# Sliding-window attention and a gated conv FFN on one core: q and k turned on VectorE, scores on 32-row tiles, two blocks per ScalarE and VectorE operation, the conv shared out among four engines, every queue's order from a table

## The chip, the cores and the metric

The kernel runs on one core of one Trainium2 chip. Five engines work side by side, each with an instruction queue of its own: TensorE (PE, matmuls into PSUM, which has eight banks of 128 x 512 f32 here), VectorE (DVE), ScalarE (ACT), GpSimd (POOL) and SyncE (SP), whose queue here issues the DMAs. The metric is the device time of one execution in microseconds; lower is better.

## What is computed

Eight batches of eight heads attend within a window of 32 positions to either side; the result goes through a feed-forward block whose gate is a three-tap convolution along the sequence.

```python
# q, k, v: 8 x 8 x 576 x 64 f32
scores = q @ k.T / sqrt(64)
mask = abs(pos[:, None] - pos[None, :]) <= 32
attn = softmax(where(mask, scores, -1e9))
x = (attn @ v).transpose(0, 2, 1, 3).reshape(8, 576, 512)
# w_in: 512 x 1024, conv_w: 3 x 1024, w_out: 1024 x 512
h = maximum(x @ w_in, 0)
conv = conv_w[0]*h[s-1] + conv_w[1]*h[s] + conv_w[2]*h[s+1]    # zero at the ends
out = (h * sigmoid(conv)) @ w_out                              # 8 x 576 x 512 f32
```

Both kernels take the sigmoid as (1 + tanh(conv/2)) / 2: the relu gives h/2, so the conv of it is conv/2, and the gate is one operation, (tanh + 1) * h/2.

## The kernel before

**Attention.** Batch by batch, two heads (a pair, `g`, 32 in all) at a time. `load_qk` (L99 to L106) brings four heads of q or k as f32 into 128 partitions, 18 rows of one head in each; `cast` (L109) turns them to bf16 on GpSimd. `job_tr` (L210) turns them: nine matmuls against the identity (L229) put 64 columns of two heads into three PSUM banks (`slot_a`, of which there is one), and one ScalarE and one VectorE copy (L236) bring the two pairs' halves out as `qT` and `kT`, with the head's 64 columns on 64 partitions. `job_sc` (L252) multiplies: nine query tiles of 64 rows against 128 keys each, for both heads of the pair, 18 matmuls on 64-row tiles (L257), again into `slot_a` (the last tile into a bank of its own). ScalarE takes the exponential of 1088 columns (L266) and of 64 (L267), VectorE multiplies with a 0/1 mask (L268). `job_av` (L270) multiplies with V, which has a column of ones for the softmax sum. V is kept twice, `ve` and, moved by 64 rows, `vo`; for batch 0 the move is VectorE's, for the others `shift_v` makes it with two DMAs (L136). A reciprocal (L292) and a multiplication (L301) on VectorE divide by the sum into `xn`. `job_xt` (L306) turns `xn` into `xT`: on TensorE for batches 0 and 1, with DMA transposes (L312) after that.

**Feed-forward.** The 4608 rows are 12 chunks of 384; three chunks lie on two batches. Per chunk and per block `m` of 128 of the 1024 hidden columns: `job_ph` (L339) runs four matmuls with `w_in` (L349) and ScalarE's relu (L360, L364, L369); `job_pc` (L371) runs the conv as three matmuls with diagonal matrices `diag_w` (L387), ScalarE's tanh from PSUM to an f32 tile in SBUF (L391), and VectorE's gate `(tn + 1) * hT` into `gT` (L392). `job_py` (L401) multiplies with `w_out`, eight matmuls for 128 rows (L405), ScalarE copies the result out (L410) and a DMA stores it (L412). Chunk 1 is done in two halves.

**Order.** Each job has a due time, written out by hand for the first batches and in a steady rhythm after that, and the jobs that must come ahead of it. `give_out` (L428) issues jobs by due time as soon as those ahead are issued. Up to a due time of 37 the instructions are held in that order on their engines (`InOrder`; these have line L87 in the profile); the DMAs and GpSimd's casts always; after that a scheduler of the framework may move instructions. Five PSUM banks (`slot_f`) rotate among the other jobs.

Of the kernel before, what the change touches and what calls it, by code (L numbers as in the profile page):

```python
# [10 lines left out]
BF16 = mybir.dt.bfloat16  # L12
AF = mybir.ActivationFunctionType
ALU = mybir.AluOpType


@with_exitstack
def kernel(
# [19 lines left out]
    NP = H // 2  # L38
# [4 lines left out]
    RP = S // 64  # L43

    consts = ctx.enter_context(tc.tile_pool(name="consts", bufs=1))
    pp = ctx.enter_context(tc.tile_pool(name="pp", bufs=1))
    apool = ctx.enter_context(tc.tile_pool(name="apool", bufs=3))
    fpool = ctx.enter_context(tc.tile_pool(name="fpool", bufs=2))
    spool = ctx.enter_context(tc.tile_pool(name="spool", bufs=3))
    psum_a = ctx.enter_context(tc.tile_pool(name="psum_a", bufs=1, space=bass.MemoryType.PSUM))  # L50
    psum_f = ctx.enter_context(tc.tile_pool(name="psum_f", bufs=5, space=bass.MemoryType.PSUM))

    NLD = 2
    NPH = NP // 2
    qkst = [[pp.tile([128, 2, RP, 64], FP32, name=f"{n}st{i}") for i in range(NPH)] for n in "qk"]
    vst = pp.tile([128, NBLK, H, 64], FP32, name="vst")
    qkb_pp = [
        [[pp.tile([128, RP, 2, 64], BF16, name=f"{n}b{i}{j}") for j in range(NPH)] for n in "qk"]
        for i in range(NLD)
    ]  # L60
    ve_pp = [pp.tile([128, NBLK, H, 65], BF16, name=f"ve{i}") for i in range(NLD)]
    vo_pp = [pp.tile([128, NBLK - 1, H, 65], BF16, name=f"vo{i}") for i in range(NLD)]
    NKT = 4
    kT_pp = [pp.tile([128, S + 2 * PAD], BF16, name=f"kT{i}") for i in range(NKT)]
    hT_pp = [pp.tile([128, MB, CH + (4 if i == 1 else 2)], BF16, name=f"hT{i}") for i in range(3)]

    w_in_sb = consts.tile([128, KC, d_ff], BF16, name="w_in_sb")
    w_out_sb = consts.tile([128, MB, d_model], BF16, name="w_out_sb")
    conv_w_sb = consts.tile([128, 3, MB], FP32, name="conv_w_sb")
    diag_w = consts.tile([128, 3, MB, 128], BF16, name="diag_w")  # L70
    ident = consts.tile([128, 128], BF16, name="ident")
    mask = consts.tile([128, 2 * S], BF16, name="mask")
    mask1 = consts.tile([128, NT, 64], BF16, name="mask1")

    fixed = tc.keep_in_program_order

    class InOrder:


        on = False  # L80

        def __init__(self, engine):
            self.engine = engine

        def __getattr__(self, name):
            do = getattr(self.engine, name)
            return (lambda *args, **kwargs: fixed(do(*args, **kwargs))) if InOrder.on else do  # L87

    vector, scalar, tensor = InOrder(nc.vector), InOrder(nc.scalar), InOrder(nc.tensor)

    def load_v(b, c):

        lo = 128 * c - PAD
        s0, s1 = max(0, lo), min(S, lo + 128)
        fixed(nc.sync.dma_start(  # L95
            vst[s0 - lo:s1 - lo, c, :, :], v[b, :, s0:s1, :].rearrange("h p d -> p h d")
        ))

    def load_qk(b, y, i):  # L99


        src = (q, k)[y][b, 4 * i:4 * i + 4, :, :]
        fixed(nc.sync.dma_start(
            qkst[y][i].rearrange("p e j d -> p e (j d)"),
            bass.AP(src.tensor, src.offset, [[RP * D, 128], [2 * S * D, 2], [1, RP * D]]),
        ))  # L106

    def cast(out_, in_):
        fixed(nc.gpsimd.tensor_scalar(  # L109
            out=out_, in0=in_, scalar1=1.0, scalar2=0.0, op0=ALU.mult, op1=ALU.add  # L110
        ))

    def load_stream(b):

        i = b % NLD
        ve, vo = ve_pp[i], vo_pp[i]

        def cast_v(c):
            cast(ve[:, c, :, 0:64], vst[:, c, :, :])
            if b == 0 and c > 0:  # L120
                vector.tensor_copy(vo[0:64, c - 1, :, :], ve[64:128, c - 1, :, :])
                vector.tensor_copy(vo[64:128, c - 1, :, :], ve[0:64, c, :, :])

        of_qk = [
            (lambda y=y, j=j: load_qk(b, y, j),
             lambda y=y, j=j: cast(qkb_pp[i][y][j].rearrange("p j e d -> p e j d"), qkst[y][j]))
            for j in range(NPH) for y in range(2)
        ]
        of_v = [(lambda c=c: load_v(b, c), lambda c=c: cast_v(c)) for c in range(NBLK)]
        return of_qk + of_v  # L130

    def shift_v(b):

        ve, vo = ve_pp[b % NLD], vo_pp[b % NLD]
        for p0, src in ((0, ve[64:128, 0:NBLK - 1]), (64, ve[0:64, 1:NBLK])):
            fixed(nc.sync.dma_start(vo[p0:p0 + 64], src))  # L136


    nc.vector.memset(vst[0:PAD, 0, :, :], 0.0)
    nc.vector.memset(vst[128 - PAD:128, NBLK - 1, :, :], 0.0)  # L140
    loads0 = list(load_stream(0))
    for ld, _ in loads0:
        ld()
    conv_w24 = consts.tile([3 * MB, 128], FP32, name="conv_w24")
    nc.scalar.dma_start(conv_w24, moe_conv_w.rearrange("k (m p) -> (k m) p", p=128))
    make_identity(nc, ident)
    ident24 = consts.tile([3 * MB, 3 * MB], FP32, name="ident24")
    nc.vector.tensor_copy(out=ident24, in_=ident[0:3 * MB, 0:3 * MB])
    nc.vector.memset(mask1, 1.0)
    nc.gpsimd.affine_select(  # L150
        out=mask1, in_=mask1, compare_op=ALU.is_ge, fill=0.0, base=0,
        pattern=[[0, NT], [-1, 64]], channel_multiplier=1,
    )
    nc.gpsimd.affine_select(
        out=mask1, in_=mask1, compare_op=ALU.is_ge, fill=0.0, base=64,
        pattern=[[0, NT], [1, 64]], channel_multiplier=-1,
    )
    nc.vector.memset(mask1[0:PAD, 0, :], 0.0)
    nc.vector.memset(mask1[128 - PAD:128, NT - 1, :], 0.0)
    for e in range(2):  # L160
        nc.vector.tensor_copy(
            out=mask[:, 512 * e:512 * e + 512], in_=mask1[:, 0:8, :].rearrange("p t x -> p (t x)")
        )
        nc.vector.tensor_copy(out=mask[:, 1024 + 64 * e:1088 + 64 * e], in_=mask1[:, 8, :])
    for t_ in ve_pp + vo_pp[0:1]:
        nc.vector.memset(t_[:, :, :, 64], 1.0)
    for t_ in kT_pp:
        nc.vector.memset(t_[:, 0:PAD], 0.0)
        nc.vector.memset(t_[:, PAD + S:], 0.0)
    nc.vector.memset(hT_pp[0][:, :, 0], 0.0)  # L170
    nc.vector.memset(hT_pp[1][:, :, HW + 1:HW + 3], 0.0)
    nc.vector.memset(hT_pp[2][:, :, CH + 1], 0.0)
    def make_diag(m):
        for kk in range(3):
            vector.tensor_scalar(
                out=diag_w[:, kk, m, :], in0=ident,
                scalar1=conv_w_sb[:, kk, m:m + 1], scalar2=None, op0=ALU.mult,
            )

    def load_weight(src, dst, rows, cast_):  # L180

        n = src.shape[1] // 2
        for x in (0, n):
            st = {}

            def load(x=x, st=st):
                t_ = fpool.tile([128, rows * n], FP32, name="wst", tag="wst")
                st[0] = t_.rearrange("p (c f) -> p c f", c=rows)
                fixed(nc.sync.dma_start(
                    st[0], src.rearrange("(c p) f -> p c f", p=128)[:, :, x:x + n]  # L190
                ))

            def casts(x=x, st=st):
                step = 512 // n
                for c in range(0, rows, step):
                    cast_(dst[:, c:c + step, x:x + n], st[0][:, c:c + step])

            yield load, casts


    def slot_a():
        return psum_a.tile([128, 1536], FP32, name="pa", tag="pa")

    def slot_f():
        return psum_f.tile([128, 512], FP32, name="pf", tag="pf")

    xT, xn = {}, {}
    state = {}

    def job_tr(g2, y):  # L210

        b, i = g2 // NPH, g2 % NPH
        nat = qkb_pp[b % NLD][y][i]
        to = []
        for g in (2 * g2, 2 * g2 + 1):
            if y == 0:
                t_ = apool.tile([128, S], BF16, name="qT", tag="qT", bufs=4)
                to.append(t_)
            else:
                t_ = kT_pp[g % NKT]  # L220
                to.append(t_[:, PAD:PAD + S])
            state["qk"[y], g] = t_

        small = b == 0
        for js in ((range(0, 4), range(4, 8), range(8, RP)) if small else (range(RP),)):
            j0, n = js[0], len(js)
            ps = slot_f() if small else slot_a()
            for j in js:
                tensor.matmul(  # L229
# [353 lines left out]
```

## Time and profile before

| | |
|---|---|
| median of 3 runs | 274.07 us (273.72 to 276.27) |
| span of the profiled execution | 271.7 us |
| PE busy | 236.4 us, 87% |
| ACT busy | 175.3 us, 65% |
| DVE busy | 160.5 us, 59% |
| POOL busy | 81.0 us, 30% |
| read from HBM, written | 32.52 MB, 9.44 MB |

The profile is of one execution. PE is the engine's matmuls, PEld its weight loads, which overlap them; a matmul's record holds its way through the array, so records in a row overlap, and the time of a job is read from starts. A group of the profile is named by line, engine, operation and tiles (`out<-in`), with the count, the busy time and the mean of one. In a timeline a line has the start, the duration and in brackets the idle time ahead of it with what ended it.

### The profile page before, as it was taken

The numbers are of one execution on the slowest core, as the hardware profiler recorded it, in microseconds if no ns is written. First come the engines' busy times: TensorE is split into PE (matmuls) and PEld (weight loads), VectorE is DVE, ScalarE is ACT, GpSimd is POOL, SyncE is SP. The second block draws the span as 40 slices with busy tenths as digits, with TensorE's granted clock in tenths as the row PEclk, the third lists the DMA queues.
The fourth block names the chain that finished last, engine by engine and source line by source line (L and its number), as shares of the span: only waits on it lengthen the run. The fifth ranks groups of instructions, "written<-read, shape, count | busy, mean of one in ns | idle before, by whom it ended". The sixth has DMA issues, their size and how long they took to land.

```text
span 271.7 us, 6447 instructions
## 1 busy us (share of the span) xinstructions
PE 236.4 (87%) x2535; PEld 143.5 (53%) x2562; DVE 160.5 (59%) x362; ACT 175.3 (65%) x370; POOL 81.0 (30%) x96
## 2 busy tenths in 40 slices
PE   1736974786999978998999999999999999999994
PEld 1625543574665544554555556565656455555551
DVE  5797385895466673765766656676666562323230
ACT  2755572585577663876777777777778567657552
POOL 5758656873026201233323432322300000000000
PEclk9999998998999997999999999999999999999998
DMA  7999999997377986399959988967546114312123
GB/s 258 256 344 358 198 296 321 224 309 164 100 183 253 222 151 165 110 287 242 208 146 319 159 196 257 294 112 177 152 121 89 40 41 109 98 39 77 41 77 116
DMA packets 70498, 49.64 MB, mean 183 GB/s; under 512 B 53676, under 2 KB 55748, under 8 KB 70468
## 3 DMA queue, kind: packets, MB, share of 16 engines
q1 hardware_dynamic: 70432, 49.22, 70.6%
q8 instruction: 20, 0.33, 0.6%
q14 instruction: 10, 0.08, 0.1%
q10 hardware_dynamic: 36, 0.01, 0.0%
HBM read 32.52 MB, written 9.44 MB: 154 GB/s over the span
## 4 chain that ended last, share of the span: by engine, by line
PE 68%; DMA 15%; DVE 5%; SPq 4%; ACT 3%; issue 2%; POOL 0%
PE pf L405 22%; PE pf L349 20%; PE pf L387 14%; DMA kst<-in_k_dram 5%; PE pa L229 4%; DMA vst<-in_v_dram 4%; PE pf L282 4%; DMA vo<-ve 3%; PE pa L257 3%; DMA xT<-xn 3%; SPq L95 2%; DVE attn L268 1%; SPq L312 1%; DVE gT L392 1%; DVE diag_w L87 1%
## 5 line engine op out<-in xcount | busy, mean ns | idle before, releaser
L392 DVE SCALAR_TENSOR_TENSOR gT<-tn,hT 128x384 bf16<-128x384 f32 (+1 forms) x96 | 55.7, 585 | 55.7 <-ACT tn L391 55.6
L349 PE MATMUL pf<-xT,w_in_sb 128*128 128x385 bf16 (+2 forms) x380 | 73.6, 317 | 4.9 <-DMA xT<-xn 3.7
L405 PE MATMUL pf<-w_out_sb,gT 128*128 128x512 bf16 x261 | 66.5, 385 | 1.7 <-issue 0.4
L387 PE MATMUL pf<-hT,diag_w 128*128 128x384 bf16 (+1 forms) x288 | 59.0, 314 | 0.7 <-ACT hT L360 0.6
L349 PEld LDWEIGHTS <-w_in_sb 128*128 128x128 bf16 x380 | 34.4, 98 | 25.9 <-issue 3.3
L410 ACT COPY y_sb<-pf 128x512 f32<-128x512 f32 x36 | 21.1, 586 | 40.8 <-PE pf L405 40.8
L391 ACT ACTIVATE tn<-pf 128x384 f32<-128x384 f32 (+1 forms) x96 | 44.9, 469 | 2.3 <-PE pf L387 1.9
L109 POOL TENSOR_SCALAR ve<-vst 128x512 bf16<-128x512 f32 x40 | 28.9, 724 | 55.2 <-DMA vst<-in_v_dram 42.9
L405 PEld LDWEIGHTS <-gT 128*128 128x128 bf16 x288 | 28.0, 99 | 30.4 <-issue 1.6
L387 PEld LDWEIGHTS <-diag_w 128*128 128x128 bf16 x288 | 26.1, 98 | 17.1 <-issue 1.2
L369 ACT ACTIVATE hT<-pf 128x385 bf16<-128x385 f32 x56 | 27.7, 496 | 10.8 <-PE pf L349 10.1
L266 ACT ACTIVATE attn<-pa 128x1088 bf16<-128x1088 f32 x26 | 27.9, 1074 | 4.7 <-PE pf L257 3.9
L109 POOL TENSOR_SCALAR qb<-qst 128x1152 bf16<-128x1152 f32 x16 | 19.9, 1242 | 26.8 <-DMA qst<-in_q_dram 26.8
L268 DVE TENSOR_TENSOR attn<-attn,mask 128x1152 bf16<-128x1152 bf16 x26 | 20.9, 804 | 10.4 <-ACT attn L267 9.6
L109 POOL TENSOR_SCALAR kb<-kst 128x1152 bf16<-128x1152 f32 x16 | 18.9, 1182 | 21.9 <-DMA kst<-in_k_dram 21.1
L301 DVE TENSOR_TENSOR xn<-pf,rec 128x320 bf16<-128x320 f32 x52 | 24.3, 486 | 0.8
L364 ACT ACTIVATE hT<-pf 128x386 bf16<-128x386 f32 x24 | 11.9, 494 | 4.4 <-PE pf L349 4.0
L282 PEld LDWEIGHTS <-attn 128*64 128x64 bf16 x520 | 10.7, 112 | 7.3 <-issue 5.6
L282 PE MATMUL pf<-ve,attn 128*64 128x65 bf16 x312 | 13.8, 199 | 0.3 <-DVE attn L268 0.3
L257 PEld LDWEIGHTS <-kT 64*128 64x128 bf16 x468 | 9.0, 95 | 7.9 <-issue 5.5
L257 PE MATMUL pa<-qT,kT 64*128 64x64 bf16 x442 | 12.3, 191 | 0.9 <-DVE kT L236 0.9
L282 PE MATMUL pf<-vo,attn 128*64 128x65 bf16 x208 | 12.9, 200 | 0.0
(84 smaller groups left out, 240.1 us busy)
## 6 DMA issues: line engine op xcount, KB each, us to landing
qst<-in_q_dram SPq DMA_DIRECT2D x16, 576.0 KB, 6.4
kst<-in_k_dram SPq DMA_DIRECT2D x16, 576.0 KB, 7.4
out_dram<-y_sb SPq DMA_DIRECT2D x36, 256.0 KB, 2.2
vst<-in_v_dram SPq DMA_DIRECT2D x24, 256.0 KB, 4.7
vo<-ve SPq DMA_DIRECT2D x14, 260.0 KB, 7.8
vst<-in_v_dram SPq DMA_DIRECT2D x16, 192.0 KB, 5.0
wst<-in_moe_w_in_dram SPq DMA_DIRECT2D x2, 1024.0 KB, 8.4
wst<-in_moe_w_out_dram SPq DMA_DIRECT2D x2, 1024.0 KB, 8.9
```

The lines of the kernel that those rows point to most:

```text
L109: fixed(nc.gpsimd.tensor_scalar(out=out_, in0=in_, scalar1=1.0, scalar2=0.0, op0=ALU.mult, op1=ALU.add))
L257: tensor.matmul(last[:, 0:64] if e * t == NT - 1 else ps[:, col(e, t):col(e, t) + 64], kT[64 * e:64 * e + 64, 64 * t:64 * t + 128], qT[64 ...
L266: scalar.activation(attn[:, 0:x], ps[:, 0:x], AF.Exp, bias=0.0, scale=scale)
L268: vector.tensor_tensor(out=attn, in0=attn, in1=mask, op=ALU.mult)
L282: tensor.matmul(pss[e][64 * j:64 * j + 64, 65 * c:65 * c + 65], attn[:, col(e, t):col(e, t) + 64], (ve if t % 2 == 0 else vo)[:, t // 2, h ...
L301: vector.tensor_tensor(out=to, in0=po[:, :, 0:64], in1=rec[:, :, None].broadcast_to([128, NBLK, 64]), op=ALU.mult,)
L349: tensor.matmul(ps[:, 0:n], w_in_sb[:, kc, m * 128:(m + 1) * 128], x_[:, kc, x0:x1], start=(kc == 0), stop=(kc == KC - 1),)
L369: scalar.activation(hT[:, m, o0:o0 + n], ps[:, 0:n], AF.Relu, bias=0.0, scale=0.5)
L387: tensor.matmul(ps[:, 0:n], diag_w[:, kk, m, :], taps(kk), start=(kk == 0), stop=(kk == 2))
L391: scalar.activation(tn[:, 0:n], ps[:, 0:n], AF.Tanh, bias=0.0, scale=1.0)
L392: vector.scalar_tensor_tensor(out=gT[c][:, m, HW * halves[0]:HW * halves[0] + n].rearrange("p (i x) -> p i x", x=HW), in0=tn[:, 0:n].rearr ...
L405: tensor.matmul(ps, gT[c][:, m, 128 * i:128 * i + 128], w_out_sb[:, m, :], start=(m == 0), stop=(m == MB - 1),)
```

## The change

Nearly all of the kernel is written anew. The mathematics, the tiles of 64 queries, the weights' layout and the w_in and w_out matmuls stay. All times of the planner are gone; a table of 839 words gives every operation of every engine, and all instructions of all queues are held in the table's order.

- **q and k.** The load of four heads is one DMA into a flat tile; the cast is given by the table to ScalarE, VectorE or GpSimd (11, 13 and 8 of 32). A VectorE transpose of 32x32 blocks of 32-bit words turns it: a word is two neighbouring columns of a head, so each head's 64 columns end on 32 partitions, as two interleaved halves `e`.
- **Scores.** Four heads at once on four 32-row tiles, two matmuls (e = 0, 1) for each tile and head, accumulated: 1,152 in place of 576. The nine tiles are taken as four and five (`h`); one exponential covers four heads (1024 or 1280 columns, 32 instead of 64), and so does one mask product, 15 of them on VectorE and 17 on GpSimd.
- **V.** 40 casts on ScalarE, VectorE and GpSimd (15, 13, 12); the move to `vo` is VectorE's for all batches, no DMA.
- **Normalising.** One reciprocal and one multiplication for four heads.
- **Feed-forward.** relu, tanh and gate take two blocks `m` at once (two banks); chunks 0 and 1 are done in halves. tanh works in place, in PSUM, where the conv lies there.
- **Conv.** For each piece of two blocks the table names a kind: P, three matmuls as before (12 whole and 3 half pieces); Y, two matmuls and VectorE adds the middle tap (9 and 5); X, ScalarE writes the first tap to PSUM and VectorE adds two (6 and 2); Z, all on GpSimd, six products and two additions, in f32 tiles in SBUF (13 and 6).
- **Output copies.** 23 on ScalarE, 13 on VectorE. 

PSUM is one tile of eight banks, and the table names the bank of each matmul group.

```diff
+ORDER = """
+s3 s1 li,2 lv,0,1 li,0 s0 s4 lq,0,1 s2 cw@0 lk,0,0 dg,2 lq,0,0 dg,6 lk,0,1 dg,4 li,1 dg,7 ci,2,p dg,0 lv,0,2 dg,5 s5
...
+th,10,0,X ph,12,0@2 th,10,1,Z ga,10,0,X xt,7,4 ye,7,1,a ph,12,2@0 ga,10,1,Z re,12,0 st,7,1 pc,10,2,Y@4 re,12,2 xt,7,3
...
+"""
...
+    def turn_qk(y, b, G):
+        src = qb_[slot(y, b, G) % NQB].bitcast(U32).rearrange("p (g d) -> p g d", g=RP)
...
+        to = to.rearrange("p s e -> p (s e)").bitcast(U32)
+        vector.transpose(to.rearrange("p (x g) -> p g x", g=RP), src)
...
+    def vo(b, c=None):
+        ve, vo = ve_[b % 2], vo_[b % 2]
+        c0, c1 = (0, NBLK - 1) if c is None else (c, c + 1)
+        vector.tensor_copy(vo[0:64, c0:c1], ve[64:128, c0:c1])
+        vector.tensor_copy(vo[64:128, c0:c1], ve[0:64, c0 + 1:c1 + 1])
...
+    def sc(b, G, h, bank):
...
+        for t in tiles_of(h):
+            for e in range(2):
+                for a in range(4):
+                    tensor.matmul(
+                        PS[:, bank + a, 64 * (t - t0):64 * (t - t0) + 64],
+                        kT[32 * a:32 * a + 32, 64 * t:64 * t + 128, e],
+                        qT[32 * a:32 * a + 32, 64 * t:64 * t + 64, e],
+                        start=(e == 0), stop=(e == 1),
+                    )
...
+    def mk(b, G, h, e):
+        attn, n = attn_of(b, G, h)
+        {"d": vector, "p": gpsimd}[e].tensor_tensor(out=attn, in0=attn, in1=mask[:, 0:4 * n], op=ALU.mult)
...
+    def pc(P, m2, kind, bank=None):
...
+        for i in range(2):
+            m = 2 * m2 + i
+            if kind in "PY":
+                kks = (0, 1, 2) if kind == "P" else (0, 2)
+                for kk in kks:
+                    tensor.matmul(
+                        ps[:, i, :], diag_w[:, m, kk, :], taps(P, m, kk),
+                        start=(kk == kks[0]), stop=(kk == kks[-1]),
+                    )
+            elif kind == "X":
+                scalar.activation(
+                    like(ps[:, i, :], P), taps(P, m, 0), AF.Copy, bias=0.0, scale=conv_w_sb[:, 0, m:m + 1]
+                )
+        if kind == "Z":
+            for kk in range(3):
+                to = ps if kk == 0 else u_[:, :, 0:width(P)]
+                for i in range(2):
+                    m = 2 * m2 + i
+                    gpsimd.tensor_scalar(
+                        out=like(to[:, i, :], P), in0=taps(P, m, kk), scalar1=conv_w_sb[:, kk, m:m + 1],
+                        scalar2=None, op0=ALU.mult,
+                    )
+                if kk:
+                    gpsimd.tensor_tensor(out=ps, in0=ps, in1=to, op=ALU.add)
+
+    def tp(P, m2, kind):
+        ps = conv_out(P, m2, kind)
+        for kk in ((1,) if kind == "Y" else (1, 2)):
+            for i in range(2):
+                m = 2 * m2 + i
+                o = like(ps[:, i, :], P)
+                vector.scalar_tensor_tensor(
+                    out=o, in0=taps(P, m, kk), scalar=conv_w_sb[:, kk, m:m + 1], in1=o,
+                    op0=ALU.mult, op1=ALU.add,
+                )
...
+    for word in ORDER.split():
+        word, _, bank = word.partition("@")
+        name, *args = word.split(",")
...
+        steps[name](*args)
```

In a word the name is the step and the numbers say which: `lq`, `lk`, `lv`, `li`, `lo` are loads of q, k, v, w_in, w_out; `cq`, `ck`, `cv`, `ci`, `co` their casts, with the engine (a, d or p) last; `tq`, `tk` the transposes; `sc`, `ex`, `mk`, `av`, `nr` scores, exponential, mask, attention times V and normalising; `xt`, `xp`, `xe` the turning of `xn`; `ph`, `re`, `pc`, `tp`, `th`, `ga` w_in, relu, conv, taps on VectorE, tanh and gate; `py`, `ye`, `st` w_out, output copy and store. `@` gives the first PSUM bank.

More of the change, by code (lines that the diff above doesn't have):

```diff
@@ L63 @@
[L63 to L80, printed above, removed]
+    pq = ctx.enter_context(tc.tile_pool(name="pq", bufs=1, space=bass.MemoryType.PSUM))
+    def tiles(n, shape, dtype, name):
+        return [pp.tile(shape, dtype, name=f"{name}{i}") for i in range(n)]
+    NST, NQB, NQT, NAT, NY = 4, 4, 3, 3, 4
+    st_ = tiles(NST, [128, RP * 64], FP32, "st")
+    qb_ = tiles(NQB, [128, RP * 64], BF16, "qb")
@@ new lines @@
+    gT_ = tiles(3, [128, MB, CH], BF16, "gT")
+    y_ = tiles(NY, [128, d_model], FP32, "y")
+    z_ = tiles(2, [128, 2, CH], FP32, "z")
+    u_ = tiles(1, [128, 2, CH], FP32, "u")[0]
+    w_in_sb = tiles(1, [128, KC, d_ff], BF16, "w_in_sb")[0]
+    w_out_sb = tiles(1, [128, MB, d_model], BF16, "w_out_sb")[0]
+    conv_w_sb = tiles(1, [128, 3, MB], FP32, "conv_w_sb")[0]
+    diag_w = tiles(1, [128, MB, 3, 128], BF16, "diag_w")[0]
+    ident = tiles(1, [128, 128], BF16, "ident")[0]
+    mask = tiles(1, [128, 4 * 5 * 64], BF16, "mask")[0]
@@ L108, in cast @@
[L108 to L145, printed above, removed]
@@ L158 @@
[L158 to L162, printed above, removed]
-        )
[L164 to L198, printed above, removed]
@@ L201, in slot_a @@
[L201 to L229, printed above, removed]
-                    ps[:, 128 * (j - j0):128 * (j - j0) + 128],
-                    nat[:, j, :, :].rearrange("p e d -> p (e d)"),
-                    ident, start=True, stop=True,
-                )
-            rows = ps[:, 0:128 * n].rearrange("p (j y x) -> p y x j", j=n, y=2)
-            for x, copy in enumerate((scalar.copy, vector.tensor_copy)):
-                copy(
-                    out=to[x].rearrange("p (x j) -> p x j", j=RP)[:, :, j0:j0 + n], in_=rows[:, x]
-                )
@@ L332, in pieces, with psum2, span @@
+    pieces = [(0, 0), (0, 1), (1, 0), (1, 1)] + [(c, None) for c in range(2, 3 * B // 2)]
+    def psum2(bank, n):
+        if n > 256:
+            return PS[:, bank:bank + 2, 0:n]
+        return PS[:, bank, :].rearrange("p (y x) -> p y x", y=2)[:, :, 0:n]
+    def span(P):
+        c, half = pieces[P]
         kind = c % 3
@@ L334, in pieces, with ph @@
         hi = CH * kind + CH + (1 if kind < 2 else 0)
-        if halves == (0, 1):
+        if half is None:
             return lo, hi
-        return (lo, lo + HW + 1) if halves == (0,) else (hi - HW - 1, hi)
-    def job_ph(c, m, halves=(0, 1)):
+        if kind == 1:
+            return (lo, lo + HW + 1) if half == 0 else (hi - HW - 1, hi)
+        return (lo, lo + HW + 1) if half == 0 else (lo + HW + 1, hi)
+    def ph(P, m2, bank):
+        where["ph", P, m2] = bank
+        c, half = pieces[P]
+        x0, x1 = span(P)
+        x_ = xT_[c // 3 % 2].rearrange("p k e s -> p k (e s)")
+        ps = psum2(bank, x1 - x0)
+        for i in range(2):
+            m = 2 * m2 + i
+            for kc in range(KC):
+                tensor.matmul(
+                    ps[:, i, :], w_in_sb[:, kc, m * 128:(m + 1) * 128], x_[:, kc, x0:x1],
+                    start=(kc == 0), stop=(kc == KC - 1),
+                )
@@ L372, in job_pc, with taps @@
+        scalar.activation(to, ps, AF.Relu, bias=0.0, scale=0.5)
+    def taps(P, m, kk):
+        c, half = pieces[P]
         kind = c % 3
         step = HW + (2 if kind == 1 else 0)
-        if m == 0 and halves[0] == 0:
-            gT[c] = fpool.tile([128, MB, CH], BF16, name="gT", tag="gT", bufs=3)
-        def taps(kk):
-            base = hT_pp[kind][:, m, kk:kk + HW]
-            return bass.AP(
-                base.tensor, base.offset + step * halves[0],
-                [list(base.ap[0]), [step, len(halves)], [1, HW]],
-            )
@@ L384, in job_pc @@
-        n = HW * len(halves)
-        ps = slot_f()
-        for kk in range(3):
-            tensor.matmul(
-                ps[:, 0:n], diag_w[:, kk, m, :], taps(kk), start=(kk == 0), stop=(kk == 2)
-            )
-        tn = spool.tile([128, CH], FP32, name="tn", tag="tn")
-        scalar.activation(tn[:, 0:n], ps[:, 0:n], AF.Tanh, bias=0.0, scale=1.0)
+        hT = hT_[kind]
+        ms = slice(m, m + 1) if isinstance(m, int) else slice(m[0], m[1] + 1)
+        base = hT[:, ms, kk:kk + HW]
@@ new lines, in taps, with width, like @@
+        off = base.offset + step * (half or 0)
+        ap = [list(base.ap[0])]
+        if not isinstance(m, int):
+            ap.append(list(base.ap[1]))
+        if half is not None:
+            ap.append([1, HW])
+        elif kind == 1:
+            ap += [[step, 2], [1, HW]]
+        else:
+            ap.append([1, CH])
+        return bass.AP(base.tensor, off, ap)
+    def width(P):
+        return CH if pieces[P][1] is None else HW
+    def like(ap, P):
+        c, half = pieces[P]
+        if half is None and c % 3 == 1:
+            names = "p y" if len(ap.shape) == 3 else "p"
+            return ap.rearrange(f"{names} (i x) -> {names} i x", i=2)
+        return ap
@@ L392, in job_pc, with ga @@
+    def ga(P, m2, kind):
+        c, half = pieces[P]
+        m = 2 * m2
+        o0 = HW * (half or 0)
         vector.scalar_tensor_tensor(
-            out=gT[c][:, m, HW * halves[0]:HW * halves[0] + n].rearrange(
-                "p (i x) -> p i x", x=HW),
-            in0=tn[:, 0:n].rearrange("p (i x) -> p i x", x=HW), scalar=1.0, in1=taps(1),
+            out=like(gT_[c % 3][:, m:m + 2, o0:o0 + width(P)], P),
+            in0=like(conv_out(P, m2, kind), P), scalar=1.0, in1=taps(P, (m, m + 1), 1),
@@ L411, in job_py, with sto @@
+    def sto(c, i, e="s"):
         r0 = c * CH + 128 * i
[L412 to L447 removed]
@@ L546 @@
[L546 to L552 removed]
+        {"s": sync, "a": scalar}[e].dma_start(out_rows[r0:r0 + 128, :], y_[(3 * c + i) % NY])
@@ new lines, in co, with cw, dg @@
+    def co(p, e):
+        copy(e, w_out_sb[:, 2 * p:2 * p + 2, :], stage(p).rearrange("p (c f) -> p c f", c=2))
+    def cw(bank):
+        tensor.matmul(PS[:, bank, 0:3 * MB], conv_w24, ident24, start=True, stop=True)
+        vector.tensor_copy(out=conv_w_sb.rearrange("p k m -> p (k m)"), in_=PS[:, bank, 0:3 * MB])
+    def dg(m):
+        vector.tensor_tensor(
+            out=diag_w[:, m, :, :], in0=ident[:, None, :].broadcast_to([128, 3, 128]),
+            in1=conv_w_sb[:, :, m:m + 1].broadcast_to([128, 3, 128]), op=ALU.mult,
+        )
@@ new lines, in s0, with s1, s2 @@
+    def s0():
+        gpsimd.memset(vst[0:PAD, 0, :, :], 0.0)
+        gpsimd.memset(vst[128 - PAD:128, NBLK - 1, :, :], 0.0)
+        scalar.dma_start(conv_w24, moe_conv_w.rearrange("k (m p) -> (k m) p", p=128))
+    def s1():
+        make_identity(nc, ident)
+        vector.tensor_copy(out=ident24, in_=ident[0:3 * MB, 0:3 * MB])
+    def s2():
+        vector.memset(mask, 1.0)
+        for base, sign in ((0, 1), (64, -1)):
+            gpsimd.affine_select(
+                out=mask[:, 0:256], in_=mask[:, 0:256], compare_op=ALU.is_ge, fill=0.0, base=base,
+                pattern=[[0, 4], [-sign, 64]], channel_multiplier=sign,
+            )
+        for i in range(1, 5):
+            vector.tensor_copy(out=mask[:, 256 * i:256 * i + 256], in_=mask[:, 0:256])
```

519 lines of the change are left out of this document (247 added, 272 removed).

## The prediction

> **What bounds the kernel now.** I read the page's busy shares first, then the busy time by stage, then the chain of waits, and last groups and short timelines for prices. The stages:
>
> ```profile
> 0.00:25.00 25.00, 10.79 (x192) 9.03 (x192) 19.71 (x68) 12.51 (x32) 16.36 (x26) 1.00 1.02 305
> 25.00:80.00 55.00, 43.47 (x514) 29.93 (x514) 35.68 (x80) 32.85 (x83) 29.05 (x33) 0.94 0.88 227
> 80.00:262.00 182.00, 176.15 (x1805) 102.00 (x1830) 104.55 (x214) 127.18 (x253) 35.56 (x38) 0.99 0.64 157
> ```
>
> The columns are the stretch, its length, then busy us of PE, weight loads, DVE, ACT and POOL, the granted clock, the DMA share and GB/s. From 80 to 262 us PE is busy 96.8%, ACT 70%, DVE 57%, POOL 20%: PE is the limit there. From 25 to 80 us PE is busy 79%, before that 43%, with the DMA engines full. The chain of waits agrees:
>
> ```profile
> PE 68%; DMA 15%; DVE 5%; SPq 4%; ACT 3%; issue 2%; POOL 0%
> ```
>
> The same chain, in order of time, gives prices of PE jobs without their pipeline tails:
>
> ```profile
> 141.98 1.46 PE pf L405 x6
> 143.44 0.49 PE pf L387 x3
> 143.93 0.50 PE pa L229 x9
> 144.43 0.66 PE pf L349 x4
> ...
> 256.07 1.73 PE pf L405 x8
> ```
>
> So a conv job (three taps, L387) is 0.49 us, nine transposes (L229) 0.50, a w_in job (L349) 0.66, a w_out job (L405) 1.73. The timeline of PE:
>
> ```profile
> 189.82 0.43 PE L257 MATMUL pa<-qT,kT 64*128 64x64 bf16 x17
> 190.07 0.19 PE L257 MATMUL pf<-qT,kT 64*128 64x64 bf16 x1
> 190.19 0.34 PE L387 MATMUL pf<-hT,diag_w 128*128 128x384 bf16 x1
> ```
>
> Eighteen score matmuls take 190.19 - 189.82 = 0.37 us, 20.6 ns each. Twenty attention-times-V matmuls took 0.44 (183.19 to 183.63).
>
> **TensorE, part by part.** Removed: 32 transposing jobs, 32 x 0.50 = 16 us. The conv is dealt out over 48 full pieces of two 128-row blocks (a piece of half width counts half): 13.5 keep three taps on PE (0.98 each, 13.2 us), 11.5 keep two (0.65, 7.5 us), 7 and 16 leave PE. Together 20.7 against 47.1 (96 x 0.49), so 26 us less. Added: the scores go from 576 matmuls on 64 rows to 1,152 on 32 rows. If instructions are the limit, as 20.6 ns for 64 columns suggests, that is 23.7 us against 11.8. Bounds: no change (four tiles side by side run twice as fast as two), to 31 us (27 ns each, 64 columns at the 0.66/4/385 us a column of L349, with no overlap at all). I take 23.7, the rate that the row has. The w_in jobs stay at 63 us, w_out at 36 x 1.73 = 62, attention-times-V 14, the first batches' transposes 2. PE's work: 186 us, against 217 before by the same prices.
>
> The Trainium skill (TensorE: Matmul & The Clock Gate, section "Wait — 56ns, not 53.3ns?") says that matmuls never start less than about 25 ns apart. The row has 20.6 ns, so the row decides; by the page the scores would be 28.8 us.
>
> **When that work can run.** The first w_in job came at 28.6 us; the new table puts it behind about the same 5 MB, and PE has 4.6 us of work in front of it. The early stage is set by loads. In the table the cast of chunk 1 of batch 3's v stands behind 16.8 MB of loads; at the 285 GB/s of the first 60 us they have landed at 2.3 + 58.9 = 61 us, and 155 us of PE work stand behind that word. Before, 3.7 us lay between the last matmul's end and the span's end. With PE as dense as in 80 to 262 (96.8%) this gives 61 + 160 + 4 = 225 us; as dense as in 25 to 80 (79%) 61 + 196 + 4 = 261. All five queues are now in a written order, and the eight PSUM banks are used in groups of 2 and 4, so I take the middle, 88%: 61 + 176 + 4 = 241.
>
> **VectorE and ScalarE.** By sums of durations. DVE loses the PSUM casts of q and k (26 us) and 17 of the 32 masks (15). Joining two blocks saves fixed parts: gates (40 x 0.95 + 16 x 0.55 = 47 against 60), normalising (30 against 39), diagonals (5). It gains 32 transposes of 576 words: 0.75 each (L236 casts as many elements in 0.75), 24 us; bounds 0.54 (the 128x576 memset) to 1.5. It gains conv taps: 42 of 384 columns at 0.55 and 18 of 192 at 0.35, 29 us; 26 casts of q, k, v (0.65 and 0.33 by the 512-wide copy of the mask, 0.29), 13 us, at most twice that; moves of V that were DMAs, 18 us (0.35 and 1.1; the 64x520 copy has 0.41), 12 to 25; 13 output copies of 0.69, 9. Sum 181 us, bounds 168 to 225. ACT falls from 191 to 164 by the same method: relu 49 to 40, tanh 49 to 40, exp 42 to 36, q/k casts from PSUM 23 to nothing, outputs 21 to 13.5, and 30 us of new casts and taps. Neither sum reaches 225, so as sums they hide behind PE.
>
> **GpSimd, and what it shares with VectorE.** This is the other path. Its rows are one-operand ones: 0.62 us for 512 columns, 1.15 for 1152, so 0.20 + 0.83 ns a column. Its new list: 8 q/k casts, 12 v casts, 6 weight casts, and 114 conv products make 76 us. There are 17 masks (19,712 columns) and 38 conv adds (24,576 columns) with two operands, of which the trace has none. Lower bound: 0.83 ns, as with one. Upper: 2.5 ns, three passes for two reads and a write. By bytes a bf16 mask moves 6 a column, as the cast does (4 in, 2 out), so 0.83; an f32 add moves 12, so 1.66. I take these: 55 x 0.20 + 16.4 + 40.8 = 68, in all 144 us (bounds 124 and 197) against 81 busy now.
>
> VectorE and GpSimd block each other, as these pairs show:
>
> ```profile
> 62.34 1.15 POOL L109 TENSOR_SCALAR qb<-qst 128x1152 bf16<-128x1152 f32 x1 [1.24 <-DMA qst<-in_q_dram]
> 62.85 0.85 DVE L392 SCALAR_TENSOR_TENSOR gT<-tn,hT 128x192 bf16<-128x192 f32 x1
> ...
> 87.75 1.15 POOL L109 TENSOR_SCALAR qb<-qst 128x1152 bf16<-128x1152 f32 x1
> 88.30 0.99 DVE L392 SCALAR_TENSOR_TENSOR gT<-tn,hT 128x384 bf16<-128x384 f32 x1 [1.54 <-ACT tn L391]
> ...
> 83.85 1.01 DVE L392 SCALAR_TENSOR_TENSOR gT<-tn,hT 128x384 bf16<-128x384 f32 x2
> 84.40 1.47 POOL L109 TENSOR_SCALAR qb<-qst 128x1152 bf16<-128x1152 f32 x1 [1.08 <-DMA qst<-in_q_dram]
> ```
>
> The gate of 192 columns is 0.35 us elsewhere; here it takes 0.85 and ends just after the cast (62.34 + 1.15 = 63.49). The one of 384 is 0.55 elsewhere, here 0.99. In the third pair the cast is the late one: 1.47 for 1.15. Gates that read tanh from PSUM leave this contest; those of the 19 GpSimd pieces (16 us), 15 masks (11), SBUF casts (13), moves of V (18) and diagonals (4) stay or join: 62 us in 90 instructions. Each meeting is free for some 0.13 us (1.47 - 1.15 = 0.32 lost of 0.46 shared), so 50 us, of which I count three quarters, 37. GpSimd has 10 us of work before the first w_in job at about 27, so 17 us idle. Behind its last piece (chunk 8, blocks 2 and 3) stand 46 us of PE work, of which about 3 can run ahead: the tanh of that piece stands ahead of later relus in ScalarE's queue, and they free PE's banks. With 4 us of end: 17 + 144 + 37 + 43 + 4 = 245.
>
> **Sum.** Two paths, 241 and 245 us of span. The profiled span of 271.7 stands 2.4 under the median of 274.07, so 243 and 247: I forecast 245.
>
> **Rivals.**
> - *The written order stalls PE everywhere as it was stalled in 25 to 80 us.* For it: a late word holds all behind it, and banks are taken in fours by scores. Against it: lost time at 79% came with a DMA share of 0.88, later 0.64. 261 + 2.4 = 263.
> - *GpSimd is the bound and the kernel becomes slower.* Place: masks and conv adds in its queue. Price: the slope of two-operand work. Its path passes 274 when GpSimd's list exceeds 274 - 2.4 - 101 = 171 us, a mean slope of 1.9 ns a column where I took 1.29. At 2.5 ns the list is 197 and the time 300. For it: no row prices this work, and VectorE's tanh and gates wait for each late piece. Against: POOL was 20% busy in the long stage. The Trainium skill (GPSIMD Engine Reference, section 3.1) gives 4497 ns for a two-operand f32 add of 2048 columns and calls one shared read port the cause, which no run here shows; by that, some 2.1 ns a column, the list is 180 us and the time 283.
> - *The order fits, and PE stays at 96.8%.* 225 + 2.4 = 227.
>
> **Numbers.** About 1% (2.7 us) is what a measurement here can tell from no change. Forecast (228 to 256): 0.46, all faster. Stalled order (256 to 271): 0.22, faster. Dense PE (below 228): 0.06, faster. GpSimd as bound: 0.26, of it 0.07 within 1% and 0.19 slower. Faster 0.74, same 0.07, slower 0.19. The range takes in the dense case at 226 and reaches into the GpSimd case to 284; some 0.04 below and 0.13 above are left out.
>
> **What would show it.** Right: no q/k matmuls against the identity, PE near 186 us by chain prices and about 88% dense from 61 us on, VectorE's transposes near 0.75 us, GpSimd's adds of 768 columns near 1.5 us. Wrong: adds of 1.9 us or more with POOL over 90% busy and PE waiting behind its tanh; score matmuls over 27 ns apart; transposes at 1.5 us, which would lift VectorE's sum to 205 and, with its waits for GpSimd, over PE's.

## The result, and the profile after

The changed kernel takes 356.99 us (median of 4, 356.84 to 358.03) against 274.12 for the kernel before: a ratio of 1.30, 95% interval 1.293 to 1.309. The forecast was 245 and the range ended at 284. The profiled execution has a span of 355.2 us. Where a kernel was timed several times, an execution that ran slower at a lower granted clock is left out of its median.

The busy time by stage, with the columns of before (length, then busy us of PE, weight loads, DVE, ACT, POOL, granted clock, DMA share, GB/s):

```profile
0.00:60.00 60.00, 23.53 (x550) 20.35 (x550) 49.27 (x84) 29.01 (x44) 39.52 (x42) 0.91 0.88 258
60.00:300.00 240.00, 158.87 (x1920) 83.78 (x1916) 146.03 (x194) 99.52 (x134) 224.07 (x159) 0.78 0.42 108
300.00:355.20 55.20, 48.11 (x257) 24.23 (x256) 31.18 (x46) 28.37 (x42) 7.73 (x6) 0.92 0.24 79
```

From 60 to 300 us POOL is busy 224 of 240 us (93%), PE 66%. GpSimd's last piece is done at 308.0 us; from 300 us on PE is busy 87%, more than any other engine, as the prediction's second path had it. The chain of waits by engine, in its line on the page:

```profile
POOL 68%; PE 16%; DVE 7%; issue 5%; ACT 2%; POOLq 1%; ACTq 0%
```

It was PE 68% before. A stretch of the same chain in order of time is GpSimd work end to end:

```profile
287.46 2.45 POOL u L172 x2
289.91 0.07 issue
289.98 1.82 POOL z L172
291.80 0.09 issue
291.89 2.48 POOL u L172 x2
```

What GpSimd does there, from the groups by line and shape (count, busy us and mean ns, idle time ahead and its cause; every instruction now has the line of one helper, L172):

```profile
L172 POOL TENSOR_SCALAR u<-hT,conv_w_sb 128x384 f32<-128x384 bf16 x52 | 69.2, 1341 | 1.3
L172 POOL TENSOR_TENSOR z<-z,u 128x768 f32<-128x768 f32 x26 | 47.4, 1823 | 2.2
L172 POOL TENSOR_SCALAR z<-hT,conv_w_sb 128x384 f32<-128x384 bf16 x26 | 40.0, 1549 | 0.5 <-DVE gT L172 0.5
L172 POOL TENSOR_TENSOR attn<-attn,mask 128x1280 bf16<-128x1280 bf16 x9 | 24.5, 2722 | 16.3 <-ACT attn L172 16.3
```

The conv products, two in 2.46 us where nothing blocks them, cost 1.23 us for 384 columns. The prediction had 0.52 (0.20 + 0.83 ns a column). All 114 products together, those of 192 columns too, are busy 142 us where 53 were summed (part of that is blocking by VectorE: the groups above have means of 1.34 and 1.55 us). The two-operand work is dearer than taken as well, 102 us against 68. And this is how the others wait for it, in the timeline:

```profile
294.44 1.80 POOL L172 TENSOR_TENSOR z<-z,u 128x768 f32<-128x768 f32 x1
296.22 3.00 POOL L172 TENSOR_SCALAR z<-hT,conv_w_sb 128x384 f32<-128x384 bf16 x2
296.27 0.84 ACT L172 ACTIVATE z<-z 128x768 f32<-128x768 f32 x1 [5.84 <-POOL z L172]
297.02 1.22 ACT L172 ACTIVATE attn<-PS 128x1280 bf16<-128x1280 f32 x1
297.15 0.96 DVE L172 SCALAR_TENSOR_TENSOR gT<-z,hT 128x768 bf16<-128x768 f32 x1 [5.13 <-ACT z L172]
298.16 1.89 PE L172 MATMUL PS<-w_out_sb,gT 128*128 128x512 bf16 x4 [3.96 <-DVE gT L172]
```

ScalarE stood 5.84 us ahead of one tanh, and an exponential that owed nothing to that piece stood behind it; VectorE's gate waited 5.13 us, and TensorE 3.96 us for that gate. Over the run ScalarE waits 97.5 us for `z`, VectorE 63.9 us for the tanh of `z`.

### The profile page after: what moved, and what is told of

It is laid out like the page before. It is cut to its first block, busy times and chain, and to the rows that moved or that the text cites. A ratio compares the mean times of both kernels' runs of the same rounds, so it can differ in the third digit from the quotient of the medians.

```text
span 355.2 us, 6627 instructions
## 1 busy us (share of the span) xinstructions
PE 230.5 (65%) x2716; PEld 128.4 (36%) x2716; DVE 226.5 (64%) x322; ACT 156.9 (44%) x220; POOL 271.3 (76%) x205
## 4 chain that ended last, share of the span: by engine, by line
POOL 68%; PE 16%; DVE 7%; issue 5%; ACT 2%; POOLq 1%; ACTq 0%
POOL z L172 29%; POOL u L172 25%; PE PS L172 16%; POOL attn L172 9%; POOL ve L172 2%; DVE diag_w L172 1%; POOL qb L172 1%; ACT attn L172 1%; DVE vo L172 1%; DVE qT L172 1%; DVE gT L172 1%; DVE mask L172 1%; DVE xn L172 1%; POOL w_out_sb L172 1%; DVE attn L172 1%
## 5 line engine op out<-in xcount | busy, mean ns | idle before, releaser
L172 PE MATMUL PS<-xT,w_in_sb 128*128 128x385 bf16 (+3 forms) x448 | 90.2, 365 | 22.2 <-ACT hT L172 12.7
L172 POOL TENSOR_SCALAR u<-hT,conv_w_sb 128x384 f32<-128x384 bf16 (+1 forms) x76 | 89.4, 1187 | 1.9
L172 PE MATMUL PS<-w_out_sb,gT 128*128 128x512 bf16 x288 | 77.0, 421 | 5.3 <-DVE gT L172 5.1
L172 PEld LDWEIGHTS <-w_in_sb 128*128 128x128 bf16 x448 | 49.1, 115 | 55.7 <-issue 40.2
L172 DVE SCALAR_TENSOR_TENSOR gT<-z,hT 128x768 bf16<-128x768 f32 (+1 forms) x19 | 23.4, 1231 | 63.9 <-ACT z L172 63.9
L172 POOL TENSOR_TENSOR z<-z,u 128x768 f32<-128x768 f32 (+1 forms) x38 | 59.7, 1572 | 3.2
L172 POOL TENSOR_TENSOR attn<-attn,mask 128x1280 bf16<-128x1280 bf16 (+1 forms) x17 | 42.5, 2497 | 24.1 <-ACT attn L172 16.3
L172 ACT ACTIVATE z<-z 128x768 f32<-128x768 f32 (+1 forms) x19 | 14.1, 742 | 97.5 <-POOL z L172 97.5
L172 POOL TENSOR_SCALAR z<-hT,conv_w_sb 128x384 f32<-128x384 bf16 (+1 forms) x38 | 52.6, 1395 | 3.0 <-ACT hT L172 2.0
L172 ACT ACTIVATE hT<-PS 128x770 bf16<-128x770 f32 (+3 forms) x56 | 39.3, 719 | 30.3 <-PE PS L172 29.1
L172 ACT ACTIVATE attn<-PS 128x1280 bf16<-128x1280 f32 (+1 forms) x32 | 35.9, 1129 | 21.4 <-PE PS L172 21.3
L172 PEld LDWEIGHTS <-gT 128*128 128x128 bf16 x288 | 29.1, 106 | 43.1 <-issue 11.5
L172 DVE SCALAR_TENSOR_TENSOR gT<-PS,hT 128x768 bf16<-128x768 f32 (+1 forms) x37 | 30.8, 842 | 16.2 <-ACT PS L172 16.1
L172 PE MATMUL PS<-qT,kT 32*128 32x64 bf16 x1152 | 18.0, 210 | 35.6 <-DVE qT L172 12.6
L172 PE MATMUL PS<-ve,attn 128*64 128x65 bf16 x384 | 21.0, 223 | 30.8 <-POOL attn L172 17.9
L172 PE MATMUL PS<-hT,diag_w 128*128 128x384 bf16 (+1 forms) x146 | 30.4, 351 | 14.0 <-ACT y L172 5.5
L172 DVE SCALAR_TENSOR_TENSOR PS<-hT,conv_w_sb,PS 128x384 f32<-128x384 bf16 (+1 forms) x60 | 30.9, 556 | 5.2 <-PE PS L172 3.7
L172 PEld LDWEIGHTS <-attn 128*64 128x64 bf16 x640 | 17.5, 135 | 45.6 <-issue 21.0
L172 ACT ACTIVATE PS<-PS 128x768 f32<-128x768 f32 (+1 forms) x37 | 25.9, 710 | 15.0 <-DVE PS L172 9.0
L172 PEld LDWEIGHTS <-kT 32*128 32x128 bf16 x1152 | 14.6, 106 | 44.9 <-issue 31.5
L172 DVE COPY vo<-ve 64x2080 bf16<-64x2080 bf16 (+1 forms) x22 | 22.8, 1036 | 7.9 <-POOL ve L172 5.8
L172 DVE TENSOR_TENSOR xn<-PS,rec 128x768 bf16<-128x768 f32 (+1 forms) x32 | 26.4, 824 | 1.1
```

Source lines behind the costliest of these rows:

```text
L172: return lambda *args, **kwargs: tc.keep_in_program_order(do(*args, **kwargs))
```

## The experiments

The theory was that GpSimd's list of work sets the time; the first rival, that the written order of all queues stalls TensorE whoever is late. Times stand beside the kernel before on the same chip, which had 271 to 277 us. Runs without a ratio are one execution each, so differences of a few us between them prove nothing alone; "less" is against the 357.0 us of the changed kernel, if nothing else is said.

**Conv off GpSimd.** All 19 pieces of kind Z become P. To find free banks, 18 of the 19 conv words were also set later in the table and 8 of their gates earlier; the other words keep their order:

```diff
-... pc,4,0,Z ... th,4,0,Z ... ga,4,0,Z
+... pc,4,0,P@6 ... th,4,0,P ... ga,4,0,P        # and 18 more
```

> The 19 GpSimd conv pieces become three matmuls each, on banks that are free at that point of the table; the result is the same. Theory (GpSimd's list sets the time): its list loses 202 us (142 of products, 60 of adds) of 271 and no longer binds; PE gains 16 pieces of 0.98 us; the time falls to 245 to 270. Rival (the written order of all queues stalls TensorE, whoever is late): GpSimd's share falls but the time stays above 320.

Measured 278.4 us (before: 270.9), 79 us less. GpSimd's busy time falls from 271 to 68. The rival's time of over 320 is not met and TensorE is 78% busy, but the order of the conv words was not kept, so this run alone does not dispose of it; the runs below that keep every word in its place do. The time stays above the expected 270 all the same, so something else is late by then.

**Masks off GpSimd**, the conv left there and every word in its place:

```diff
-mk,0,0,0,p
+mk,0,0,0,d        # and 16 more
```

> The 17 GpSimd masks go to VectorE, nothing else. Theory (GpSimd's list sets the time): the list loses 42 us, VectorE gains 17 of 0.8, the time falls by 35 to 45, to about 315 to 322. Rival (written order): less than 10 us, as the masks' places in the table stay.

Measured 328.2 us, 29 less; GpSimd's busy time 232, 39 less. That is less than the 35 to 45 expected, but three quarters of what the list lost came back as time, where the rival had under 10.

**What makes a product dear.** The products differ from the casts, from which their price was taken, in several ways: a factor read from SBUF per partition, bf16 input, f32 output, and one arithmetic operation where the cast has two (times 1, plus 0).

```diff
-scalar1=conv_w_sb[:, kk, m:m + 1], scalar2=None, op0=ALU.mult
+scalar1=0.5, scalar2=None, op0=ALU.mult                                        # constant factor
+scalar1=conv_w_sb[:, kk, m:m + 1], scalar2=0.0, op0=ALU.mult, op1=ALU.add      # with an addition
```

> GpSimd's 114 conv products multiply with the constant 0.5 in place of the per-partition weight read from SBUF, so the pieces given to GpSimd leave the conv weights out. If the per-partition operand makes a product of 384 columns cost 1.23 us, it falls to 0.5 to 0.6 and the time by 70 to 90 us, to 270 to 290. If the bf16 input or the f32 output makes it, the product stays at 1.2 and the time at 357.

Measured 344.7 us, 12 less and far from the 270 to 290 expected. Two unblocked products of 384 take 2.30 us, 1.15 each: the operand per partition is worth 0.08 us of the 0.7 in question.

The tiles `z` and `u` in bf16:

> The tiles of GpSimd's conv (products and sums) are bf16 in place of f32. If the f32 output makes the price, products fall to about 0.5 to 0.6 us and the time to 270 to 300. If the bf16 input makes it, they stay at about 1.2 us, and the time changes only by what the additions gain, less than 30 us.

Measured 350.4 us; the 384-column products have a mean of 1.33 us (into `u`) where they had 1.34. So it is not the output type.

> GpSimd's conv products get a second operation, + 0.0, as its casts have one; the result is the same. If the one-operation form is what makes a product of 384 columns cost 1.23 us (1.15 with a constant factor) where a cast's rows would give 0.51, it falls to 0.5 to 0.6 and the time by 60 to 90 us. If the bf16 input or the f32 output makes it, nothing changes: 350 to 360.

Measured 296.1 us, 61 us less, from one operand that changes no value; every word is in its place. GpSimd's timeline of this run:

```profile
225.98 1.14 POOL L172 TENSOR_SCALAR u<-hT,conv_w_sb 128x384 f32<-128x384 bf16 x2
227.20 1.81 POOL L172 TENSOR_TENSOR z<-z,u 128x768 f32<-128x768 f32 x1
```

A product is now 0.57 us. So the form with one operation is the slow one. To keep bf16 input apart from the form, the same was then done the other way round, on the kernel with the lighter VectorE (below): GpSimd's f32 casts lost their addition.

```diff
-gpsimd.tensor_scalar(out=out_, in0=in_, scalar1=1.0, scalar2=0.0, op0=ALU.mult, op1=ALU.add)
+gpsimd.tensor_scalar(out=out_, in0=in_, scalar1=1.0, scalar2=None, op0=ALU.mult)
```

> On the lighter-VectorE kernel GpSimd's casts lose their second operation (+ 0.0): times 1 alone, the result is the same. If the one-operation form is the slow one whatever the type, the 1152-column cast goes from 1.15 to about 2.9 to 3.5 us (as 0.57 went to 1.23 for 384) and the time rises by a few us at most, as GpSimd has room (20% busy). If the form is slow only with bf16 input, the cast stays at 1.15.

GpSimd's casts in the groups of the two kernels, first with the addition, then without:

```profile
L171 POOL TENSOR_SCALAR qb<-st 128x1152 bf16<-128x1152 f32 x21 | 25.7, 1224 | 33.6 <-DMA st<-in_k_dram 17.5 <-DVE xn L171 7.7 <-DMA st<-in_q_dram 5.9
```

```profile
L171 POOL TENSOR_SCALAR qb<-st 128x1152 bf16<-128x1152 f32 x21 | 67.3, 3212 | 4.3 <-DMA st<-in_k_dram 2.0 <-DMA st<-in_q_dram 1.5 <-DVE kT L171 0.8
```

1.22 becomes 3.21 us with f32 input: the form decides, not the type. Two unblocked casts of the second kernel give the price:

```profile
36.93 1.49 POOL L171 TENSOR_SCALAR ve<-vst 128x512 bf16<-128x512 f32 x1
38.38 3.12 POOL L171 TENSOR_SCALAR qb<-st 128x1152 bf16<-128x1152 f32 x1
```

That is some 2.55 ns a column, (3.12 - 1.49) / 640, against 0.83 with the addition. The time was 271.0 us beside 261.9 without the edit on the same chip, 9 us more where a few at most were expected: the late casts of the first loads hold up the start, and the first w_in job begins at 38.7 us in place of 27.9.

**Both repairs, and both moves.** First the addition and the masks on VectorE together, then conv and masks both off GpSimd:

> The products with + 0.0 (296 us) and the 17 masks on VectorE, nothing else changed. GpSimd's list falls from 211 to about 169 us and VectorE's sum rises by 13. Theory (296 is still GpSimd's list): 268 to 280, with VectorE now as late as GpSimd. Rival (VectorE, busy 78% at 296 us, already sets the time there): 290 to 300.

Measured 275.7 us (before: 276.4). With GpSimd's list short enough (174 us busy), the table's conv on GpSimd costs, as far as single runs can tell, no more than conv on TensorE:

> Both of the first two edits: GpSimd keeps 8 q/k casts, 12 v casts and 5 weight casts. Theory: PE (202 us by chain prices) or VectorE (its 181 by my sum, 24 more for transposes at 1.25, 14 for masks) binds; 235 to 260. Rival (written order): above 300.

Measured 272.1 us (before: 270.9). The rival's 300 is not met, but neither are the 235 to 260 of the theory: without any arithmetic of the conv or masks on GpSimd the new kernel only draws level. Where it is held:

```profile
30.00:150.00 120.00, 92.33 (x1530) 59.12 (x1529) 102.56 (x163) 72.89 (x108) 12.16 (x15) 0.96 0.82 215
```

VectorE is busy 85% of this stretch, TensorE 77%. That led to two runs on VectorE.

**The transposes.** They take 1.25 us, not the 0.75 of the prediction.

```diff
-vector.transpose(to.rearrange("p (x g) -> p g x", g=RP), src)
+vector.transpose(to.rearrange("p (g x) -> p g x", g=RP), src)
```

> On the kernel with conv on TensorE and masks on VectorE, the transposes write each 32x32 block to 32 neighbouring words in place of words 72 bytes apart; q's and k's positions are then in another order, so the attention is over other rows. If the stride makes a transpose cost 1.25 us, it falls to 0.65 to 0.75 and the time by 8 to 16 us, as VectorE is the busiest engine from 30 to 150 us. If it is two cycles for each 32-bit word, 1.25 stays and the time too.

Measured 266.1 us, 6 less than the 272.1 of the kernel with both moves (the kernel before had 272.4 and 270.9 beside them). The edit puts q's and k's positions in another order and not those of mask and V, so this run leaves out the right pairing of rows; the amount of work is the same. The two kernels' groups, the stride first:

```profile
L172 DVE STREAM_TRANSPOSE qT<-qb 128x576 uint32<-128x576 uint32 x16 | 19.9, 1246 | 0.1
```

```profile
L172 DVE STREAM_TRANSPOSE qT<-qb 128x576 uint32<-128x576 uint32 x16 | 12.3, 766 | 0.3
```

The stride of the writes costs 0.48 us a transpose, 15 us in all on VectorE, of which 6 show in the time of one run each.

**Work taken off VectorE** in the early stage, casts to GpSimd (in the form with two operations), conv pieces 0 to 6 to TensorE alone, output copies to ScalarE:

```diff
-... pc,0,1,Y@6 ... cq,1,0,d ... tp,0,1,Y ... ye,1,1,d        # and more of each
+... pc,0,1,P@6 ... cq,1,0,p ...              ye,1,1,a
```

> On the kernel with conv on TensorE and masks on VectorE: VectorE's 26 casts go to GpSimd, the X and Y conv pieces of piece 0 to 6 become P (TensorE, no taps on VectorE), the output copies of chunks 0 to 3 go to ScalarE. VectorE loses some 16 us of casts, 12 of taps, 4 of copies, nearly all before 150 us; TensorE gains some 6. Theory (VectorE holds TensorE up before 150 us): 250 to 262. Rival (the written order, not a busy engine, keeps TensorE at 77% there): 268 to 275.

Measured 260.2 us beside 272.4 for the kernel before. The same stretch:

```profile
30.00:150.00 120.00, 100.71 (x1699) 65.37 (x1708) 89.26 (x124) 81.20 (x117) 33.32 (x38) 0.96 0.90 237
```

VectorE loses 13 us, TensorE gains 8 of busy time (77% to 84%) and the span loses 12. So VectorE did hold TensorE up there, as far as three moves made together can show it: leaving out the taps also takes a VectorE step out of the way from conv to tanh, some 3 of TensorE's 8 us are the taps that it took over, by the chain prices, and what each move is worth was not tested. Timed in rounds:

> The lighter-VectorE kernel once more, timed against the kernel before: 258 to 262, a ratio near 0.95.

261.9 us against 274.7, with a ratio of 0.961 (0.952 to 0.970): faster than both kernels.

**Two attempts to go on.**

> On the lighter-VectorE kernel (260 us): the seven GpSimd pieces of piece 7 to 10 are given back to GpSimd, products with + 0.0. TensorE, 95% busy from 150 us on, loses 7 x 0.98 us; GpSimd, idle there, gains 7 of about 7 us. Theory (a queue with room takes work for nothing): 253 to 257. Rival (VectorE's gates of these pieces and GpSimd block each other and the tanh comes late in a fixed order): 260 to 268.

260.6 us, a ratio of 0.944 (0.936 to 0.953) on its chip, where the run without these pieces had 260.2 in one execution and, on another chip, 261.9 and 0.961. A gain of 1 or 2% is neither shown nor excluded; the 253 to 257 us expected are not met. The stretch in which the seven pieces lie, without and with them:

```profile
150.00:210.00 60.00, 57.11 (x683) 31.45 (x690) 43.54 (x66) 37.88 (x50) 2.58 (x4) 1.00 0.29 79
```

```profile
150.00:210.00 60.00, 50.51 (x666) 27.60 (x672) 51.90 (x62) 36.93 (x48) 58.31 (x58) 0.97 0.30 66
```

GpSimd goes from 4% to 97% busy: an idle queue became the bound of its own stretch, VectorE gained 8 us, and TensorE stood idle for 9 us of the stretch in place of 3, about what the seven pieces had spared it.

> On the lighter-VectorE kernel (260 us): the loads of q and k come ahead of those of w_in and v, their casts likewise, and VectorE's eight diagonal products stand behind the first four transposes in place of ahead of them. The first scores begin some 4 us earlier than at 13 to 14 us. If the start is on the path, 255 to 258; if loads of V set the first attention anyway, 259 to 261.

> Both of the two edits above on the lighter-VectorE kernel. If both gain, 249 to 254; if the gains are of the same wait, no better than the better one.

270.5 and 269.2 us (ratios of 0.981 and 0.977), but these two say nothing of the start: the edit also put the load `lo,2` ahead of the cast `ci,2`, which empties the same staging tile, so columns 512 to 767 of w_in held values of w_out and that cast waited 15 us for a later load. Done again with that load in its place:

> On the lighter-VectorE kernel: the loads of q and k come first, then w_in and v with their casts behind those of q and k, VectorE's eight diagonal products stand behind the first four transposes, and each w_out load stays behind the cast that empties its staging tile. If the start is on the path: first scores near 10 us in place of 13 to 14 and 255 to 258. If V and w_in set the first w_in job: within 1.5 us of the kernel without the edit.

264.0 us, a ratio of 0.964 (0.956 to 0.971), against 261.9 and 0.961 without the edit, which the intervals do not tell apart. The first scores start at 10.2 us instead of 15.5, and then VectorE's moves of V wait 4.17 us for a v cast that now stands behind two casts of w_in in GpSimd's queue, the second of which waited 8.5 us for its load. The first w_in job begins at 31.9 us in place of 27.9. The wait was moved; the start is not shown to be worth anything in this order.

## Why the prediction was wrong

**The path was right, the term of the conv products was not.** The step that failed is the price of the 114 conv products in GpSimd's list: 53 of its 144 us, 142 measured. The prediction's second path, 17 us idle + GpSimd's list + 37 us blocked + 43 us behind the last piece + 4 us, is the shape of the profile. Put in what GpSimd was busy, blocked time included (271): 17 + 271 + 47 = 335 of the 355 measured. The 47 us behind the last piece are met (308.0 to 355.2); the other 20 are idle time, 37 us before the last piece's end where 17 were summed, 24 of them ahead of masks.

The list was taken as 144 us, with 37 for blocking 181, 90 less than was measured. By parts, with blocking inside them, the products are 89 us over, the two-operand work 34 and the casts and the rest 4; against these 127 stand the 37 set aside for blocking. Of the 89, the form explains about 62: with the addition the products are busy 80 us. The rest is blocking and 0.57 us where the cast's row gave 0.52.

"114 conv products make 76 us" with the casts took 0.83 ns a column. That price was read from GpSimd's casts, which are `tensor_scalar` with two operations; the products have one. The name of the instruction in the profile is the same, TENSOR_SCALAR. I checked dtype and operand count for the two-operand work and gave bounds; to the products I gave one value and no bounds, because they seemed to have a row. The runs with and without the addition (357 to 296 us, 1.23 to 0.57; 1.22 to 3.21 for casts) show this cause.

**Two-operand work** was mis-sized in the same direction. Taken by bytes: 0.83 ns a bf16 column, 1.66 an f32 one. Measured without blocking: 2.60 and 2.12 us for masks of 1280 and 1024 columns, 1.81 for adds of 768; less 0.20 us each that is about 1.9 and 2.1 ns, so bytes matter little (in bf16 the adds of 768 have a mean of 1.65 us where they had 1.82). Busy 102 us against 68. The Trainium skill (GPSIMD Engine Reference, section 3.1) had the f32 price: 4497 ns for 2048 columns, by estimate 2.1 ns a column after the same 0.20 us. The trace agrees with its 2.1 ns. The rival that GpSimd is the bound named the right path, and its 283 us came closer than the forecast; it still fell 74 us short, because it priced the products as the forecast did. With the products alone repaired the kernel takes 296.

**The chance of 0.26** for GpSimd as the bound was too low for a path that already stood 4 us above the other one at my own prices. The range could not hold 357: it ended at 284, and even the list's upper bound of 197 gave only 300.

**TensorE's terms.** Transposes gone, as forecast. Scores were taken at 20.6 ns each; forty take 0.42 us:

```profile
252.80 0.48 PE L172 MATMUL PS<-qT,kT 32*128 32x64 bf16 x40
253.22 0.99 PE L172 MATMUL PS<-xT,w_in_sb 128*128 128x385 bf16 x5
```

That is 10.5 ns each: four tiles run twice as fast as two, the lower bound. So 1,152 scores cost what 576 did, 12 us less than summed. The code goes round the tiles in turn, so by these figures the starts on one tile are 42 ns apart with four tiles and 41 with two. The Trainium skill (TensorE: Matmul & The Clock Gate, section "Wait — 56ns, not 53.3ns?") has matmuls start never less than about 25 ns apart. Across tiles this does not hold here; on one tile no run tests it. The gain did not show in the time, as GpSimd set it.

**VectorE's terms.** The transposes were 1.25 us, inside the bounds of 0.54 and 1.5 but not the value taken: 16 us more. The terms that the prediction lists for VectorE (47, 30, 11 and 4 that stay, 24, 29, 13, 18 and 9 that join) add up to 185 us, not 181, which changes no step of it. That VectorE's sum would hide behind TensorE was wrong in the early stage, where it mattered: the sum was compared over the whole run, and 103 of its 212 us lie between 30 and 150 us (in the kernel without conv and masks on GpSimd). In the changed kernel itself blocking shows too: the move of V of 2080 columns has a mean of 1.35 us there and 0.70 without GpSimd's conv and masks.

**The stalled order** (263 us) is not needed for the step from 357: with every word in its place the two repairs give 276 us. What is left by then may still be the order. With conv and masks moved the kernel takes 272 us and TensorE is busy 77% from 30 to 150 us, close to this rival's 79%. Taking work off VectorE brings 260 and 84% there. What holds the other 16% was not tested, and how much a different order would gain was not tried beyond the start.

## What to carry to other kernels

Take an instruction's price only from a row with the same form, operation count included, and where no row has it, bound it even if the name is the same. Compare engine sums stage by stage, not over the run: an engine that hides overall can hold the others up for 120 us. An idle queue is worth using only up to what it can do in that stretch; in a fixed order its lateness becomes the lateness of every queue that waits for it.

## What was not expected of the hardware

- GpSimd's `tensor_scalar` with one operation takes 2.55 ns a column, with a second one (+ 0.0) 0.83: 3.12 against 1.15 us for 1152 columns.
- VectorE's 32x32 transpose of 576 words takes 0.77 us with neighbouring writes and 1.25 with writes 72 bytes apart.
- Matmuls of 64 columns on four 32-row tiles start 10.5 ns apart, on two 64-row tiles 20.6.
- TensorE's granted clock and its busy share often fell together: 0.78 from 60 to 300 us, where PE was busy 66%, and 1.00 from 150 to 210 us in the 260 us kernel, where it was busy 95%. That waiting lowers the clock is not shown: with the one-operation casts it was 1.00 from 30 to 150 us at 78% busy.
